# Attention scores: two 64x64 products on opposite quarters of the TensorE array in place of one 128-row product with zero-padded q

## The chip, the cores and the metric

The kernel runs on one core of one Trainium2 chip. The metric is the device time of one execution in microseconds (us). The core has five engines with their own instruction queues: TensorE (PE, with its weight loads shown apart as PEld), VectorE (DVE), ScalarE (ACT), GpSimd (POOL) and SyncE (SP), which here only issues DMAs.

## The reference, cut to what matters

Three layers are chained: a windowed attention, a routed layer with one expert per token, and a second routed layer with two experts per token. Only the attention is touched by the change:

```python
B, H, S, D = q.shape                      # 4, 8, 576, 64
scores = scale * np.matmul(q, k.transpose(0, 1, 3, 2))
mask_plain = (rel >= 0) & (rel < 32)                       # heads 0..3
mask_dil = (rel >= 0) & (rel < 128) & (rel % 4 == 0)       # heads 4..7
scores = np.where(masks[None], scores, -1e9)
attn = np.exp(scores - scores.max(-1, keepdims=True))
attn = attn / (attn.sum(-1, keepdims=True) + 1e-9)
return np.matmul(attn, v)
```

All data is fp32.

## The kernel before

**Units.** The attention is cut into 16 units, each one batch and a pair of heads. The 128 partitions of the transposed q and k tiles (`qT`, `kT`) hold 64 channels of the first head and 64 of the second. A unit has 576 positions in 9 blocks of 64 queries; block n needs only 96 keys (`kT[:, 64*n:64*n+96]`). For heads with the dilated mask the positions are reordered, so that the same 64 by 96 blocks serve.

**Stages of a unit.** The class `Attention` has one method for each stage, and the table `plan` in the main function fixes their order on PE, by a string such as `A0 D0 A1 B0 A2 D1 B1 A3 X E X D2` for each turn of the loop:

- `A0` to `A3` (`qk_T`): three PE transposes into a PSUM bank `tp`, then an eviction into `qT` (parts 0 and 1) or `kT` (parts 2 and 3). It works three units ahead of the values. The eviction of q also scales by -0.125.
- `B0`, `B1` (`scores`): five and four score blocks into a PSUM bank `s`; then on DVE one masked add and minimum for each block (L192, two instructions each, into `sm` and `nmax`); then on ACT one exponential for each block (L196), whose sum goes to `ssum`; then DVE makes the reciprocals `rs` (L198, L199) and POOL multiplies by them (L200).
- `D0` to `D2` (`probs_T`): PE transposes the probabilities into a bank `pt`, and ACT (DVE for part 1) evicts them into `pT` (L215, L217).
- `E` (`values`): products with v into `po0` and `po1`; ACT evicts into `xT`.
- `X`: routing work of earlier batches that is put in between (`logits`, `rows`, tables). `rows` transposes tokens into a bank `tp`, copies them to `xr` (two buffers) and writes them to `xs` in DRAM by a DMA on SP.

PE's order is written out by hand. The order on DVE, ACT, POOL and SP is made by the scheduler of the tile framework at build time.

**The zero padding.** Both heads' scores of a block come from one PE product: the stationary operand is q of the block with queries and heads interleaved, 128 columns, in which column (query, head) holds zeros in the other head's 64 rows. So `qT` is `[128, 576, 2]`, its other half is filled with zeros once by POOL (L82, L83; four buffers, two fills each), and each q eviction is two instructions, one for each head's 64 partitions (L176; L174 on ACT for the first two units). The partitions of the scores are (query, head) interleaved; the eviction of `pT` sorts them by head.

**What follows the attention.** `kT`, `qT` and the masks lie in the pool `at_fix`, the loaded q and k in `at_ld`, both at the right end of the on-chip memory. `first_tile` gives this memory to the first expert weights (pool `w_hl_a`, four tiles `whi`, `wlo` of 8 KB per partition), and `P.load(4)` issues their four DMAs of 1 MB each on SP (L494). `reuse_waits="tile"` makes each new tile wait only for the old tiles in its own bytes. After the attention the first layer starts with `logits_l`, `rows_l` and the expert tile `X[0]`, and then the experts of both layers follow with three-pass products (L454 to L456).

Of the kernel before, what the change touches and what calls it, by code (L numbers as in the profile page):

```python
# [8 lines left out]
F32 = mybir.dt.float32  # L9
# [3 lines left out]
ALU = mybir.AluOpType  # L13
AF = mybir.ActivationFunctionType
# [11 lines left out]
class Attention:  # L26
# [7 lines left out]
    def __init__(self, ctx, early, tc, bank, q, k, v, ident, xT):  # L34
        self.tc, self.nc, self.bank = tc, tc.nc, bank
        self.q, self.k, self.v = q, k, v
        self.ident, self.xT = ident, xT
        self.B, self.H, self.S, self.D = q.shape
        nc = self.nc
        self.NB = self.S // 64  # L40

        self.vp = ctx.enter_context(tc.tile_pool(name="at_v", bufs=2))
        self.wk = ctx.enter_context(tc.tile_pool(name="at_wk", bufs=2))
        fix = early.enter_context(tc.tile_pool(name="at_fix", bufs=1, side="right"))
        self.ld = early.enter_context(tc.tile_pool(name="at_ld", bufs=2, side="right"))
        NB, R = self.NB, self.S // 4


        ip = fix.tile([128, 1], I32, name="ip")
        nc.gpsimd.iota(ip, pattern=[[0, 1]], base=0, channel_multiplier=1)  # L50
        nc.vector.tensor_single_scalar(ip, ip, 1, op=ALU.logical_shift_right)
        fi = fix.tile([128, 2], F32, name="fi")
        nc.vector.tensor_copy(fi[:, 0:1], ip)
        nc.vector.tensor_scalar(fi[:, 1:2], fi[:, 0:1], 32.0, None, op0=ALU.add)
        col = fix.tile([128, 96], F32, name="col")
        nc.gpsimd.iota(col, pattern=[[1, 96]], base=0, channel_multiplier=0, allow_small_or_imprecise_dtypes=True)
        inner = fix.tile([128, 96], F32, name="mask_in")
        nc.vector.tensor_scalar(inner, col, fi[:, 0:1], BIG, op0=ALU.is_le, op1=ALU.mult)
        nc.vector.tensor_scalar(col, col, fi[:, 1:2], BIG, op0=ALU.is_gt, op1=ALU.mult)
        nc.vector.tensor_max(inner, inner, col)  # L60
        first = fix.tile([128, 96], F32, name="mask_first")
        nc.vector.tensor_copy(first, inner)
        nc.vector.memset(first[:, :32], BIG)
        self.mask = [[first] + [inner] * (NB - 1), [first] + [inner] * (NB - 1)]
        rowbig = fix.tile([128, 1], F32, name="rowbig")
        for n in range(1, NB):
            for b in range(R, self.S, R):
                i0, c0 = b - 64 * n, b - 64 * n + 32
                if c0 <= 0 or i0 >= 64:
                    continue  # L70
                m = fix.tile([128, 96], F32, name=f"mask_{n}")
                nc.gpsimd.tensor_copy(m, inner)
                nc.vector.tensor_scalar(rowbig, fi[:, 0:1], float(i0), BIG, op0=ALU.is_ge, op1=ALU.mult)
                nc.vector.tensor_scalar(m[:, :min(c0, 96)], m[:, :min(c0, 96)], rowbig, None, op0=ALU.max)
                self.mask[1][n] = m
        self.kT, self.qT = [], []
        for i in range(4):
            t = fix.tile([128, 32 + self.S], F32, name=f"kT{i}")
            nc.vector.memset(t[:, :32], 0.0)
            self.kT.append(t)  # L80
            t = fix.tile([128, self.S, 2], F32, name=f"qT{i}")
            nc.gpsimd.memset(t[0:64, :, 1], 0.0)  # L82
            nc.gpsimd.memset(t[64:128, :, 0], 0.0)  # L83
            self.qT.append(t)
        self.tiles, self.vt, self.pT, self.p = {}, {}, {}, {}

    def unit(self, m):
# [53 lines left out]
    def qk_T(self, m, part):  # L141

        nc = self.nc
        b, hp, dil = self.unit(m)
        nm, g = "qk"[part // 2], part % 2
        src = self.tiles[nm, m]
        pt = self.bank("tp")[:, :288].rearrange("p (c a) -> p c a", c=3)
        for c in range(3):
            nc.tensor.transpose(pt[:, c, :], src[:, 3 * g + c, :], self.ident[:96, :96])
        if nm == "k":  # L150
            kT = self.kT[m % 4]
            if dil:
                o = kT[:, 32:].rearrange("p (h s c a) -> p h s c a", h=2, s=2, c=3)[:, g]
                i_ = pt.rearrange("p c (a s) -> p s c a", s=2)
            else:
                o = kT[:, 32 + 288 * g:320 + 288 * g]
                i_ = pt.rearrange("p c a -> p (c a)")
            if m < 2 and g == 1:
                nc.scalar.activation(o, i_, AF.Copy)
            else:  # L160
                nc.vector.tensor_copy(o, i_)
            return
        qT = self.qT[m % 4]

        for h in range(2):
            rows = slice(64 * h, 64 * h + 64)
            if dil:
                o = qT[rows, :, h].rearrange("p (h s c a) -> p h s c a", h=2, s=2, c=3)[:, g]
                i_ = pt[rows].rearrange("p c (a s) -> p s c a", s=2)
            else:  # L170
                o = qT[rows, 288 * g:288 * g + 288, h]
                i_ = pt[rows].rearrange("p c a -> p (c a)")
            if m < 2 and h == 1:
                nc.scalar.activation(o, i_, AF.Copy, scale=-0.125)  # L174
            else:
                nc.vector.tensor_scalar(o, i_, -0.125, None, op0=ALU.mult)  # L176

    def scores(self, m, part):
        nc, NB = self.nc, self.NB
        b, hp, dil = self.unit(m)  # L180
        qT, kT = self.qT[m % 4], self.kT[m % 4]
        if part == 0:
            self.p[m] = (self.wk.tile([128, NB, 96], F32, name="sm", bufs=4),
                         [self.wk.tile([128, NB], F32, name=nm, bufs=4) for nm in ("nmax", "ssum", "rs")])
        sm, (nmax, ssum, rs) = self.p[m]
        n0, n1 = ((0, 5), (5, NB))[part]
        ps = self.bank("s")[:, :480].rearrange("p (n c) -> p n c", n=5)
        for n in range(n0, n1):
            nc.tensor.matmul(ps[:, n - n0, :], lhsT=qT[:, 64 * n:64 * n + 64, :].rearrange("p q h -> p (q h)"),
                             rhs=kT[:, 64 * n:64 * n + 96], start=True, stop=True)  # L190
        for n in range(n0, n1):
            nc.vector.tensor_tensor_reduce(out=sm[:, n, :], in0=ps[:, n - n0, :], in1=self.mask[dil][n],  # L192
                                           scale=1.0, scalar=3.0e38, op0=ALU.add, op1=ALU.min,
                                           accum_out=nmax[:, n:n + 1])
        for n in range(n0, n1):
            nc.scalar.activation(sm[:, n, :], sm[:, n, :], AF.Exp, bias=nmax[:, n:n + 1], scale=-1.0,  # L196
                                 accum_out=ssum[:, n:n + 1])
        nc.vector.tensor_scalar(rs[:, n0:n1], ssum[:, n0:n1], 1.0e-9, None, op0=ALU.add)  # L198
        nc.vector.reciprocal(rs[:, n0:n1], rs[:, n0:n1])  # L199
        nc.gpsimd.tensor_tensor(out=sm[:, n0:n1, :], in0=sm[:, n0:n1, :],  # L200
                                in1=rs[:, n0:n1, None].to_broadcast([128, n1 - n0, 96]), op=ALU.mult)

    def probs_T(self, m, part):
        nc, NB = self.nc, self.NB
        if part == 0:
            self.pT[m] = self.wk.tile([96, NB, 128], F32, name="pT", bufs=3)
        p, pT = self.p[m][0], self.pT[m]
        n0 = 3 * part
        pt = self.bank("pt")[:96, :384].rearrange("p (n c) -> p n c", n=3)
        for n in range(n0, n0 + 3):  # L210
            nc.tensor.transpose(pt[:, n - n0, :], p[:, n, :], self.ident)
        o = pT[:, n0:n0 + 3].rearrange("p n (h q) -> p n h q", h=2)
        i_ = pt.rearrange("p n (q h) -> p n h q", h=2)
        if part == 1:
            nc.vector.tensor_copy(o, i_)  # L215
        else:
            nc.scalar.activation(o, i_, AF.Copy)  # L217

    def values(self, m):
        nc, NB, S = self.nc, self.NB, self.S  # L220
# [1441 lines left out]
```

## Time and profile before

| | us |
|---|---|
| median of 3 runs (795.01 to 796.71) | 796.49 |
| the profiled execution, its own time | 798.44 |
| its span in the trace | 796.6 |
| PE busy | 752.0 (94%) |
| DVE busy | 362.3 (45%) |
| ACT busy | 310.3 (39%) |
| POOL busy | 272.8 (34%) |

The span is the time from the first to the last instruction that the profiler recorded; the execution's own time is 1.84 us longer. A busy share over the whole span hides the stages: the attention takes about the first 125 us, and there DVE and ACT are far busier than their averages. PE records overlap (an instruction starts before the one ahead has ended), so a busy share of PE near 100% does not mean that it works at its peak.

### The profile page before, as it was taken

The page shows a single profiled execution, that of the slowest core. Times are in us where ns is not written, and L with a number is a line of the kernel's source. Part 1 is how long each engine was busy: PE and PEld are TensorE (multiplying, and loading weights), DVE is VectorE, ACT ScalarE, POOL GpSimd, SP SyncE. Part 2 cuts the span into 40 slices and gives each one's busy share as a digit, 9 for nine tenths or more (in the row PEclk, how much of TensorE's full clock was granted, in tenths as well). Part 3 has the DMA queues.
Part 4 walks back from the last instruction along what each step waited for, and adds up shares of the span by engine and source line. Part 5 has one row for each costly group of instructions (what it writes and reads, how often), then busy time and mean ns, then how long its engine had stood idle before and what let it go on. Part 6 is the DMA issues. An engine that isn't in the chain of part 4 may idle for free.

```text
span 796.6 us, 13971 instructions
## 1 busy us (share of the span) xinstructions
PE 752.0 (94%) x5280; PEld 647.1 (81%) x5280; DVE 362.3 (45%) x1237; ACT 310.3 (39%) x826; POOL 272.8 (34%) x259
## 2 busy tenths in 40 slices
PE   7998985998998999899999999999999999999994
PEld 7877873866886887789898898997997988988983
DVE  8977894547425636944432441440531531220110
ACT  5778761215214433314433442442532433332120
POOL 6322120024234424134504325434333445544011
PEclk9999997999999999999999999999999999999998
DMA  7978536289679898243725516515445444313122
GB/s 182 182 167 217 127 109 252 68 312 345 247 236 318 294 352 289 70 127 103 202 99 142 142 54 155 130 64 144 130 131 92 118 153 69 115 26 43 17 27 28
DMA packets 109336, 121.06 MB, mean 152 GB/s; under 512 B 42384, under 2 KB 65424, under 8 KB 109264
## 3 DMA queue, kind: packets, MB, share of 16 engines
q1 hardware_dynamic: 98144, 95.95, 38.2%
q0 software_dynamic: 9808, 22.86, 14.7%
q10 hardware_dynamic: 1312, 1.31, 0.5%
q8 instruction: 43, 0.70, 0.4%
q14 instruction: 29, 0.24, 0.1%
HBM read 96.50 MB, written 23.59 MB: 151 GB/s over the span
## 4 chain that ended last, share of the span: by engine, by line
PE 75%; DVE 10%; DMA 5%; ACT 5%; issue 2%; POOL 1%; SPq 0%; POOLq 0%; DVEq 0%; ACTq 0%
PE pt L454 10%; PE pt L456 10%; PE pt L455 10%; PE s L454 5%; PE s L455 5%; PE po L456 5%; PE s L456 5%; PE po L454 5%; PE po L455 5%; ACT sm L196 4%; PE s L755 3%; PE pt L763 3%; PE tp L734 2%; DMA wlo<-in_moe_w_dram 2%; DMA wraw<-in_moe_w_dram 2%
## 5 line engine op out<-in xcount | busy, mean ns | idle before, releaser
L449 POOL TENSOR_TENSOR wlo<-wraw,whi 128x512 fp32r<-128x512 f32 x76 | 109.3, 1497 | 159.2 <-ACT whi L448 139.4
L454 PE MATMUL pt<-whi,hh 128*128 128x512 f32 (+1 forms) x320 | 129.6, 405 | 0.0
L449 DVE TENSOR_TENSOR wlo<-wraw,whi 128x512 fp32r<-128x512 f32 x84 | 79.0, 954 | 110.0 <-ACT whi L448 106.0
L456 PE MATMUL pt<-whi,hl 128*128 128x512 f32 (+1 forms) x320 | 126.1, 394 | 0.0
L455 PE MATMUL pt<-wlo,hh 128*128 128x512 f32 (+1 forms) x320 | 126.0, 394 | 0.0
L448 ACT ACTIVATE whi<-wraw 128x512 fp32r<-128x512 f32 x160 | 91.1, 622 | 57.1 <-PE po L455 17.1
L1224 POOL DMA_INDIRECT out_dram<-y,sidx x40 | 63.3, 1582 | 112.4 <-ACT y L1436 106.8
L727 POOL DMA_INDIRECT xg<-xs,gidx x51 | 52.0, 1019 | 129.4 <-PE tp L734 36.7
L456 PE MATMUL s<-xh,wlo 128*128 128x256 f32 (+1 forms) x256 | 72.7, 284 | 0.0
L455 PE MATMUL s<-xl,whi 128*128 128x256 f32 (+1 forms) x256 | 72.6, 283 | 0.0
L454 PE MATMUL s<-xh,whi 128*128 128x256 f32 (+1 forms) x256 | 72.5, 283 | 0.0
L456 PE MATMUL po<-xh,wlo 128*128 128x352 f32 x224 | 72.5, 324 | 0.0
L454 PE MATMUL po<-xh,whi 128*128 128x352 f32 x224 | 72.4, 323 | 0.0
L455 PE MATMUL po<-xl,whi 128*128 128x352 f32 x224 | 72.2, 322 | 0.0
L456 PEld LDWEIGHTS pt<-whi,hl 128*128 128x128 f32 (+1 forms) x320 | 58.4, 183 | 15.8
L455 PEld LDWEIGHTS pt<-wlo,hh 128*128 128x128 f32 (+1 forms) x320 | 58.6, 183 | 13.7
L454 PEld LDWEIGHTS pt<-whi,hh 128*128 128x128 f32 (+1 forms) x320 | 58.6, 183 | 13.3
L1436 ACT ACTIVATE y<-pt,slots 128x512 f32<-128x512 f32 (+1 forms) x40 | 27.5, 688 | 99.5 <-PE pt L456 88.7
L1422 DVE SCALAR_TENSOR_TENSOR hl<-po,hh 128x352 fp32r<-128x352 f32 x56 | 29.3, 522 | 69.5 <-ACT hh L1421 69.4
L196 ACT ACTIVATE sm<-sm,nmax 128x96 f32<-128x96 f32 x144 | 51.9, 361 | 22.3 <-DVE nmax L192 22.0
L449 DVE TENSOR_TENSOR xl<-tp,xh 128x512 fp32r<-128x512 f32 (+1 forms) x40 | 26.4, 663 | 70.2 <-ACT xh L448 54.5
L200 POOL TENSOR_TENSOR sm<-sm,rs 128x480 f32<-128x480 f32 (+1 forms) x32 | 29.2, 912 | 76.9 <-DVE nmax L192 51.3
(406 smaller groups left out, 1506.8 us busy)
## 6 DMA issues: line engine op xcount, KB each, us to landing
wraw<-in_moe_w_dram SPq DMA_DIRECT2D x40, 1024.0 KB, 5.5
whi<-in_moe_w_dram SPq DMA_DIRECT2D x12, 1024.0 KB, 7.6
wlo<-in_moe_w_dram SPq DMA_DIRECT2D x12, 1024.0 KB, 9.7
out_dram<-zt SPq DMA_DIRECT2D x46, 128.0 KB, 4.3
xs<-xr SPq DMA_DIRECT2D x13, 256.0 KB, 3.2
v<-in_v_dram SPq DMA_DIRECT2D x7, 432.0 KB, 5.4
xs<-xg SPq DMA_DIRECT2D x11, 256.0 KB, 4.4
qld<-in_q_dram SPq DMA_DIRECT2D x8, 288.0 KB, 3.5
```

The costliest lines, as they stand in the source:

```text
L196: nc.scalar.activation(sm[:, n, :], sm[:, n, :], AF.Exp, bias=nmax[:, n:n + 1], scale=-1.0, accum_out=ssum[:, n:n + 1])
L200: nc.gpsimd.tensor_tensor(out=sm[:, n0:n1, :], in0=sm[:, n0:n1, :], in1=rs[:, n0:n1, None].to_broadcast([128, n1 - n0, 96]), op=ALU.mult)
L448: nc.scalar.activation(hi, src, AF.Copy)
L449: (eng or nc.vector).tensor_tensor(out=lo, in0=src, in1=hi.bitcast(F32), op=ALU.subtract)
L454: nc.tensor.matmul(out, lhsT=a[0], rhs=b[0], start=start, stop=False)
L455: nc.tensor.matmul(out, lhsT=a[0], rhs=b[1], start=False, stop=False)
L456: nc.tensor.matmul(out, lhsT=a[1], rhs=b[0], start=False, stop=stop)
L727: gather.last = nc.gpsimd.indirect_dma_start(out=xg, out_offset=None, in_=xs[:n, :], in_offset=bass.IndirectOffsetOnAxis(ap=idx, axis=0))
L755: nc.tensor.matmul(ph[:, 128 * f:128 * f + 128], lhsT=w[:, c, 128 * f:128 * f + 128], rhs=self.x[:, c], start=c == 0, stop=c == KC - 1)
L1224: s = nc.gpsimd.indirect_dma_start(out=out, out_offset=bass.IndirectOffsetOnAxis(ap=idx, axis=0), in_=y, in_offset=None, compute_op=ALU.add)
L1422: nc.vector.scalar_tensor_tensor(hl[1][:, f, s_], in0=ph, scalar=0.0, in1=hl[0][:, f, s_].bitcast(F32), op0=ALU.max, op1=ALU.subtract)
L1436: nc.scalar.activation(y[:n], py, AF.Copy, scale=slots2[:n, 2, j:j + 1])
```

## The change

Each score block is made by two products, one per head: rows 0 to 63 of q and k into partitions 0 to 63 of the bank, and rows 64 to 127 into partitions 64 to 127. The partitions of the scores are now sorted by head, so the query of a partition is its number modulo 64, and the sorting at the eviction of `pT` goes. `qT` shrinks from `[128, 576, 2]` to `[128, 576]`, the zero fills go, and q is evicted by one instruction over 128 partitions, like k.

```diff
-        nc.vector.tensor_single_scalar(ip, ip, 1, op=ALU.logical_shift_right)
+        nc.vector.tensor_single_scalar(ip, ip, 63, op=ALU.bitwise_and)
...
-            t = fix.tile([128, self.S, 2], F32, name=f"qT{i}")
-            nc.gpsimd.memset(t[0:64, :, 1], 0.0)
-            nc.gpsimd.memset(t[64:128, :, 0], 0.0)
-            self.qT.append(t)
+            self.qT.append(fix.tile([128, self.S], F32, name=f"qT{i}"))
...
-        for h in range(2):
-            rows = slice(64 * h, 64 * h + 64)
-            if dil:
-                o = qT[rows, :, h].rearrange("p (h s c a) -> p h s c a", h=2, s=2, c=3)[:, g]
-                i_ = pt[rows].rearrange("p c (a s) -> p s c a", s=2)
-            else:
-                o = qT[rows, 288 * g:288 * g + 288, h]
-                i_ = pt[rows].rearrange("p c a -> p (c a)")
-            if m < 2 and h == 1:
-                nc.scalar.activation(o, i_, AF.Copy, scale=-0.125)
-            else:
-                nc.vector.tensor_scalar(o, i_, -0.125, None, op0=ALU.mult)
+        t = self.kT[m % 4][:, 32:] if nm == "k" else self.qT[m % 4]
+        if dil:
+            o = t.rearrange("p (h s c a) -> p h s c a", h=2, s=2, c=3)[:, g]
+            i_ = pt.rearrange("p c (a s) -> p s c a", s=2)
+        else:
+            o = t[:, 288 * g:288 * g + 288]
+            i_ = pt.rearrange("p c a -> p (c a)")
+        scale = 1.0 if nm == "k" else -0.125
+        if m < 2 and g == 1:
+            nc.scalar.activation(o, i_, AF.Copy, scale=scale)
+        elif nm == "k":
+            nc.vector.tensor_copy(o, i_)
+        else:
+            nc.vector.tensor_scalar(o, i_, scale, None, op0=ALU.mult)
...
-            nc.tensor.matmul(ps[:, n - n0, :], lhsT=qT[:, 64 * n:64 * n + 64, :].rearrange("p q h -> p (q h)"),
-                             rhs=kT[:, 64 * n:64 * n + 96], start=True, stop=True)
+            for h in range(2):
+                rows = slice(64 * h, 64 * h + 64)
+                nc.tensor.matmul(ps[rows, n - n0, :], lhsT=qT[rows, 64 * n:64 * n + 64], rhs=kT[rows, 64 * n:64 * n + 96],
+                                 start=True, stop=True)
...
-        o = pT[:, n0:n0 + 3].rearrange("p n (h q) -> p n h q", h=2)
-        i_ = pt.rearrange("p n (q h) -> p n h q", h=2)
+        o = pT[:, n0:n0 + 3]
         if part == 1:
-            nc.vector.tensor_copy(o, i_)
+            nc.vector.tensor_copy(o, pt)
         else:
-            nc.scalar.activation(o, i_, AF.Copy)
+            nc.scalar.activation(o, pt, AF.Copy)
```

The scheduler makes the other engines' order anew. Two places matter below. The first is VectorE in the middle of the attention, between the end of one unit's masks and the start of the next unit's: `rs` are the reciprocals, `qT` the q evictions, `sm,nmax` a mask instruction with the minimum behind it. Before:

```order
L161 COPY kT_207<-tp 128x288
L198 TENSOR_SCALAR rs<-ssum 128x4
L199 RECIPROCAL rs<-rs 128x4
L176 TENSOR_SCALAR qT_194<-tp 64x288 x4
L192 ISA sm,nmax<-s,mask_first 128x96
L192 ISA nmax 128x1
```

And now, at the same place:

```order
L158 COPY kT_201<-tp 128x288
L184 TENSOR_SCALAR rs<-ssum 128x4
L185 RECIPROCAL rs<-rs 128x4
L160 TENSOR_SCALAR qT_194<-tp 128x288 x2
L178 ISA sm,nmax<-s,mask_first 128x96
L178 ISA nmax 128x1
```

Four q evictions ahead of the next unit's first mask have become two, and nothing else has moved there.

The second is SyncE's queue at the end of the attention, where the last `v` tile has been loaded, one token tile is written (`xs<-xr`), and the first four weight tiles are issued; the square brackets name the counters on which an instruction waits (`DMAHW` for an earlier DMA, the rest by engine). Before:

```order
L135 DMA v_1965<-in_v_dram 96x2x128 [waits DMAHW1_49]
L687 TENSOR_LOAD eri_a [waits DVE_49]
L827 DMA xs<-xr 128x512 [waits DMAHW2_49,DVE_49]
L494 DMA whi<-in_moe_w_dram 128x4x512 [waits DMAHW3_49,DVE_49]
...
L494 DMA wlo<-in_moe_w_dram 128x4x512 [waits DMAHW4_49,PE_49]
...
L494 DMA whi<-in_moe_w_dram 128x4x512 [waits DMAHW5_49]
...
L494 DMA wlo<-in_moe_w_dram 128x4x512 [waits DMAHW6_49,PE_49]
L827 DMA xs<-xr 128x512 [waits DMAHW7_49,DVE_49]
```

And now:

```order
L132 DMA v_2060<-in_v_dram 96x2x128 [waits DMAHW1_49]
L812 DMA xs<-xr 128x512 [waits DMAHW2_49,DVE_49]
L672 TENSOR_LOAD eri_a [waits DVE_49]
L479 DMA whi<-in_moe_w_dram 128x4x512 [waits DMAHW3_49,PE_49]
...
L479 DMA wlo<-in_moe_w_dram 128x4x512 [waits DMAHW4_49]
...
L479 DMA whi<-in_moe_w_dram 128x4x512 [waits DMAHW5_49,DVE_49,Pool_49]
...
L479 DMA wlo<-in_moe_w_dram 128x4x512 [waits DMAHW6_49,PE_49]
L812 DMA xs<-xr 128x512 [waits DMAHW7_49,DVE_49]
```

The DVE wait, which stood on the first weight tile, now stands on the third. The smaller `qT` moves the other tiles of `at_fix` and `at_ld` by 9,216 bytes per partition, while the weight tiles stay where they were: the first weight tile's bytes held the masks and some of `kld`, `kT` and `qT`, and now they hold only loaded q and k; the third now covers the masks. The DVE wait is that for the last mask instruction of the last unit (L192); the PE wait of the first tile is now that for the last transposes of a loaded k tile.

## Rows read from the trace of the kernel before

**Rows 1.** Windows of the whole core: us, busy time of each engine, clock, DMA.

```profile
core 0: us, PE busy (x) PEld busy (x) DVE busy (x) ACT busy (x) POOL busy (x), PEclk, DMA share, GB/s
0.00:116.30 116.30, 102.81 (x1263) 91.48 (x1263) 96.19 (x556) 83.32 (x355) 37.39 (x78) 0.99 0.70 164
116.30:134.00 17.70, 8.40 (x128) 6.79 (x131) 9.45 (x50) 3.99 (x13) 3.02 (x3) 0.83 0.78 282
134.00:796.60 662.60, 640.78 (x3892) 548.84 (x3892) 256.63 (x634) 223.00 (x459) 232.37 (x178) 0.98 0.50 146
```

**Rows 2.** Windows of 10 us in the attention, with the same columns.

```profile
10.00:20.00 10.00, 7.46 (x56) 6.96 (x55) 8.23 (x53) 7.55 (x38) 3.37 (x8) 0.83 0.64 154
30.00:40.00 10.00, 9.63 (x134) 9.05 (x133) 8.79 (x47) 8.12 (x36) 3.38 (x5) 1.00 1.10 205
```

**Rows 3.** The chain that ended last, to 116.3 us, shares by line.

```profile
by line: ACT sm L196 28.0%; PE s L189 9.7%; DVE qT L176 9.6%; PE tp L149 6.1%; DVE sm L192 5.6%; PE pt L211 3.9%; issue 3.6%; ACT xT L251 2.6%; DVE rs L198 2.3%; PE po L247 1.8%; PE tp L833 1.7%; PE tp L821 1.6%; POOL qT L83 1.6%; PE tp L84
```

**Rows 4.** The same chain in order of time: start, us, what.

```profile
8.45 0.62 POOL qT L83
9.09 1.52 DVE mask L74
10.68 1.90 ACT sm L196 x10
...
114.00 1.91 ACT sm L196 x10
```

**Rows 5.** Groups by line and shape, 0 to 200 us: busy us, mean ns.

```profile
L189 PE MATMUL s<-kT,qT 128*128 128x96 f32 x288 | 37.8, 278 | 0.0
L176 DVE TENSOR_SCALAR qT<-tp 64x288 f32<-64x288 f32 x60 | 27.2, 454 | 7.8 <-PE tp L149 6.7
L161 DVE COPY kT<-tp 128x288 f32<-128x288 f32 x30 | 13.5, 451 | 0.0
L82 POOL MEMSET qT<- 64x576 f32 x4 | 2.6, 646 | 0.1
```

**Rows 6.** Timeline of one unit's scores: start us, us, engine, line.

```profile
57.39 1.88 DVE L176 TENSOR_SCALAR qT<-tp 64x288 f32<-64x288 f32 x4 [1.19 <-PE tp L149]
57.52 0.41 PE L149 MATMUL tp<-ident,qld 96*128 96x96 f32 x3
57.77 1.28 PE L189 MATMUL s<-kT,qT 128*128 128x96 f32 x10
58.88 0.41 PE L149 MATMUL tp<-ident,kld 96*128 96x96 f32 x3
59.30 0.26 DVE L192 CUSTOM_DVE_ANT_0 sm<-s,mask_first 128x96 f32<-128x96 f32 x1
59.60 0.38 ACT L196 ACTIVATE sm<-sm,nmax 128x96 f32<-128x96 f32 x1 [1.33 <-DVE nmax L192]
```

**Rows 7.** Timeline of PE around the values of one unit.

```profile
38.97 0.41 PE L149 MATMUL tp<-ident,kld 96*128 96x96 f32 x3
39.31 1.27 PE L229 MATMUL po<-pT,v 96*64 96x64 f32 x36
40.51 0.53 PE L211 MATMUL pt<-ident,sm 128*96 128x128 f32 x3
```

**Rows 8.** Timeline of SP and DVE at the attention's end.

```profile
112.07 0.36 SPq L827 DMA_DIRECT2D xs<-xr  x1
116.29 0.43 SPq L494 DMA_DIRECT2D whi<-in_moe_w_dram  x1
121.04 13.78 SPq L827 DMA_DIRECT2D xs<-xr  x4
...
116.01 0.25 DVE L192 CUSTOM_DVE_ANT_0 sm<-s,mask_in 128x96 f32<-128x96 f32 x1
...
133.16 1.31 DVE L826 COPY xr<-tp 128x512 f32<-128x512 f32 x2 [7.43 <-DMA xs<-xr]
```

More of the change, by code (lines that the diff above doesn't have):

```diff
@@ L149, in qk_T @@
             nc.tensor.transpose(pt[:, c, :], src[:, 3 * g + c, :], self.ident[:96, :96])
-        if nm == "k":
-            kT = self.kT[m % 4]
-            if dil:
-                o = kT[:, 32:].rearrange("p (h s c a) -> p h s c a", h=2, s=2, c=3)[:, g]
-                i_ = pt.rearrange("p c (a s) -> p s c a", s=2)
-            else:
-                o = kT[:, 32 + 288 * g:320 + 288 * g]
-                i_ = pt.rearrange("p c a -> p (c a)")
-            if m < 2 and g == 1:
-                nc.scalar.activation(o, i_, AF.Copy)
-            else:
-                nc.vector.tensor_copy(o, i_)
-            return
-        qT = self.qT[m % 4]
-        for h in range(2):
-            rows = slice(64 * h, 64 * h + 64)
-            if dil:
-                o = qT[rows, :, h].rearrange("p (h s c a) -> p h s c a", h=2, s=2, c=3)[:, g]
-                i_ = pt[rows].rearrange("p c (a s) -> p s c a", s=2)
-            else:
-                o = qT[rows, 288 * g:288 * g + 288, h]
-                i_ = pt[rows].rearrange("p c a -> p (c a)")
-            if m < 2 and h == 1:
-                nc.scalar.activation(o, i_, AF.Copy, scale=-0.125)
-            else:
-                nc.vector.tensor_scalar(o, i_, -0.125, None, op0=ALU.mult)
+        t = self.kT[m % 4][:, 32:] if nm == "k" else self.qT[m % 4]
[12 more added lines that the diff above has]
+            nc.vector.tensor_scalar(o, i_, scale, None, op0=ALU.mult)
     def scores(self, m, part):
@@ L211, in probs_T @@
             nc.tensor.transpose(pt[:, n - n0, :], p[:, n, :], self.ident)
-        o = pT[:, n0:n0 + 3].rearrange("p n (h q) -> p n h q", h=2)
-        i_ = pt.rearrange("p n (q h) -> p n h q", h=2)
+        o = pT[:, n0:n0 + 3]
         if part == 1:
-            nc.vector.tensor_copy(o, i_)
+            nc.vector.tensor_copy(o, pt)
         else:
-            nc.scalar.activation(o, i_, AF.Copy)
+            nc.scalar.activation(o, pt, AF.Copy)
     def values(self, m):
```

## The prediction

> **What bounds the kernel now.** I read first the windows that cut the span at the two places the change can reach [rows 1]. From 134 us on PE is busy 640.8 of 662.6 us with the experts' products, which the change leaves alone: whatever is won or lost must be won or lost before, and is then carried to the end as a shift. To 116.3 us runs the attention, and no engine is full there: PE 102.8, DVE 96.2, ACT 83.3 of 116.3 us. From 116.3 to 134 us PE is busy only 8.4 of 17.7 us.
>
> Then the chain of waits for the attention [rows 3]. It passes from engine to engine: the exponentials on ACT (L196) hold 28%, the score products on PE (L189) 9.7% or 11.3 us, the q evictions on DVE (L176) 9.6% or 11.2 us. The last two are what the change touches. In order of time [rows 4] the first group of exponentials starts at 10.68 us and that of the sixteenth unit at 114.00, so 15 periods of 6.89 us on average.
>
> The timeline of one unit shows how a period closes [rows 6]. The two transposes of q feed four evictions on DVE from 57.39 to 59.27 us; the mask instructions of the new scores stand behind them in DVE's queue and start at 59.30; ACT has waited 1.33 us and starts its exponentials at 59.60. PE meanwhile made the five score blocks of this part from 57.77 to 58.88 us.
>
> Last, the attention's end [rows 8]. The first expert weights are issued at 116.29 us, when the last unit's last masks (the row at 116.01) are done. They are four DMAs of 1 MB, and the token tiles issued from 121.04 us queue behind them. DVE waits 7.43 us for the first of these to land and goes on at 133.16, and PE waits for DVE. So the end of the four weight transfers is what starts the rest of the kernel.
>
> **The change, part by part.**
>
> *Start.* The eight zero fills take about 8 x 0.65 us on POOL [rows 5], the last from 8.45 to 9.07 us, and the fills and index rows queued behind them run later still. The mask instruction at 9.09 us on DVE took 1.52 us [rows 4], six times what a mask of the scores takes (0.26 us, [rows 6]), and the first exponential waited for it until 10.68. Now POOL has 5.2 us less to do ahead of it, and the instruction should take some 0.25 us: 1.3 us less. Two of four q evictions leave DVE's queue here, 0.9 us more, but the first scores' own products come at about the same time as now, which eats most of that. I take 1.6 us; bounds 0.3 (the products come as late as the masks do now) and 2.2 (both in full).
>
> *q evictions.* Sixty instructions of 454 ns over 64 partitions become thirty over 128. The k eviction has exactly this shape and takes 451 ns [rows 5], so half of 27.2 us goes, 0.9 us of DVE in each unit. In the unit of [rows 6] the second eviction can start when its transposes end (57.52 + 0.41 = 57.93) and ends at 58.38, 0.9 us before 59.27.
>
> *Score products.* fp32 products run as two passes, so five blocks are ten records: 58.88 - 57.77 = 1.11 us, or 111 ns each [rows 6]; nine blocks take 2.0 us. Now there are twice as many, each with 64 weight columns. The nearest row is that of the values, 64 weight columns with the two column halves in turn: 36 records in 40.51 - 39.31 = 1.20 us, 33 ns each [rows 7]. They move 64 columns where the scores move 96, so the bounds are 33 and 50 ns; I take 40. Then there is the change of array shape: from transposes to values PE took 39.31 - 38.97 = 0.34 us [rows 7] where a transpose part otherwise takes 57.77 - 57.52 = 0.25 [rows 6], so 0.09 us, and each unit gets four more such changes, two for each part. The five blocks then take 20 x 0.040 + 0.09 = 0.89 us in place of 1.11, and PE wins 2.0 - 36 x 0.040 - 0.36 = 0.2 us a unit; without the cost of the changes and at 33 ns it would be 0.8 us.
>
> *A period.* The masks need the last product of their part. It ends at 57.77 + 0.89 plus a record's tail of 0.17 (1.28 - 1.11), about 58.85 us, which is later than the evictions (58.38). So the masks start 0.45 us earlier, and everything behind them with them. ACT has room: in 30 to 40 us, its fullest stretch, it is busy 8.12 of 10 us [rows 2], so a period of 5.9 us could lose 1.1. I take 0.45 us for all 15 periods, 6.8 us. Bounds: 0.2 (PE sets all of them) gives 3.0, and 0.75 (DVE sets them, products at 33 ns) gives 11.0. The chain gives a check: half of its 11.2 us of evictions and a fifth of its 11.3 us of score products are 7.9 us, a little of which other waits will take back.
>
> *Other edits.* The mask's index costs the same instruction. The eviction of pT reads in another order over the same elements; I take nothing for it.
>
> *Weights.* With the smaller `qT` the first two of the four weight DMAs no longer wait for the last masks, only for transposes that are long done, so they follow the token tile issued at 112.07 us, at about 112.5 instead of 116.29 [rows 8]: 3.8 us. The other two still wait for the masks, at 116.2 us, but four transfers and the first tile behind them take 133.16 - 116.29 = 16.9 us, half of that 8.4, so the first two are still moving until 120.9 and no gap opens. The tile that lands at 133.16 is issued at 121.04 and still stands behind the weights when they end 3.8 us earlier. I take 3.8 us. Bounds: 1 (the early pair shares the engines with the late loads of v) and 4.8 (the copy ahead of the tile at 112.07 us moves up too).
>
> *Sum.* 1.6 + 6.8 + 3.8 = 12.2 us. The profiled execution took 798.44 us (span 796.6 and 1.84 around it), 1.95 above the median of the runs; I take the difference from the median: 796.49 - 12.2 = **784.3 us**.
>
> **A rule that speaks against it.** [Rows 7] shows 0.09 us for a change of array shape. The Trainium skill, TensorEngine Tiling (Array Packing), Key Properties, says that changing the tiling mode drains TensorE; if a drain were a record's whole length less its pace, 278 - 111 = 0.17 us, the trace would bear out only half of it. The same page, Gotcha 1: PSUM Pressure, says that different row tiles cannot write the same bank at one time; no row of this kernel shows two row tiles, so what that would do is the second rival below.
>
> **The rivals.**
>
> *Shape changes cost double.* At 0.17 us, the record's length of 278 ns [rows 5] less its pace, PE loses 36 x 0.040 + 0.68 - 2.0 = 0.12 us a unit instead of winning 0.2, and the masks start 0.37 us earlier. For it speaks that four changes stand in each unit; against it the 0.09 us measured. With 0.1 us a period in the mean: 1.6 + 1.5 + 3.8 = 6.9 us, 789.6 us. Chance 0.12.
>
> *The two halves don't overlap (slower).* Both write one PSUM bank, from different row halves. If one waits for the other, a product costs 2 x 33 = 67 ns [rows 7], nine blocks 36 x 0.067 + 0.36 = 2.8 us, and PE, which is busy 9.63 of 10 us in 30 to 40 us [rows 2], needs 0.8 us more a unit: 12 us over 15 periods, less 5.4 from start and weights, is 6.6 slower, 803 us. It decides from 56 ns a product on (36 x 0.056 + 0.36 = 2.36, 0.36 above now; times 15 that eats the 5.4). Against it: they write different partitions, as the values' halves do. Chance 0.06.
>
> *The early weights bring nothing*, because the tiles land no sooner for another reason: 8.4 us, 788.1 us. Chance 0.10.
>
> *The clock falls.* In 10 to 20 us the granted clock is 0.83 of full speed behind a stretch with little PE work (7.46 busy of 10, [rows 2]), while it is 1.00 in 30 to 40 us. With less work in each period PE could drop to its lower level, 1.2 of 2.4 GHz, now and then. At 0.9 over the attention, a tenth of 103 us of PE work, the gain is nearly gone: about 794 to 797 us. Against it: the periods shrink with the work. Chance 0.04.
>
> **How the numbers follow.** The forecast has 0.66, a gain beyond 17 us 0.02. From the bounds, the sum runs from 0.3 + 3.0 + 1.0 = 4.3 to 2.2 + 11.0 + 4.8 = 18 us, 778.5 to 792.2 us. I give 779 to 791.5, which holds the forecast but for its tails and most of the first and third rivals: about 0.8. A measurement of this kernel tells a difference from about 0.2%, 1.6 us. Faster: 0.66 + 0.02 + 0.12 + 0.10 + half of 0.04 = 0.92; same 0.02; slower 0.06.
>
> **What the profile would show.** Right: 30 q evictions of about 450 ns over 128 partitions; no fill of qT, and first exponentials at about 9 us; 20 score records in 0.8 to 0.9 us; periods of about 6.4 us; two weight DMAs issued right behind a token tile and before the last masks, and DVE's wait for the first token tile behind them ending near 121 us. Wrong: score records that start 56 ns apart or more, a clock below 1.00 in the middle of the attention, or the two early weight DMAs issued with the others.

## The result, and the profile after

The changed kernel took 789.38 us (median of five runs, 787.83 to 791.85) beside 796.71 us for the kernel before on the same chip: a ratio of 0.9905, 95% interval 0.9881 to 0.9928. Run once more in a later group it took 786.67 us beside 797.72, 0.9873 (0.9831 to 0.9915). So 7 to 11 us were won where 12.2 were forecast; the time lies in the range given. The profiled execution took 788.40 us, its span is 786.5 (before: 798.44 and 796.6). Three of the thirteen executions of one version below (e7), the profiled one among them, were slower than the rest by 10 us or more, so its median is that of the other ten, and its trace, whose first 65 us ran at half pace, is read behind 90 us.

Windows cut at the same two places as in [rows 1], the end of the last masks and PE's return:

```profile
0.00:109.48 109.48, 99.77 (x1551) 82.40 (x1551) 81.97 (x526) 82.55 (x352) 32.50 (x70) 1.00 0.74 175
109.48:125.00 15.52, 8.35 (x128) 6.74 (x131) 9.40 (x50) 4.26 (x14) 3.03 (x3) 0.86 0.88 321
125.00:786.50 661.50, 640.03 (x3892) 547.20 (x3892) 257.37 (x634) 222.73 (x459) 231.64 (x178) 0.99 0.51 147
```

Of the 10.1 us between the two spans 6.8 lie in the attention and 2.2 in the stretch behind it; the last stretch is 1.1 us shorter, with the same instructions. DVE's work to the end of the attention fell from 96.19 to 81.97 us. The groups that answer to [rows 5], 0 to 200 us:

```profile
L175 PE MATMUL s<-kT,qT 64*64 64x96 f32 x576 | 30.8, 248 | 0.0
L158 DVE COPY kT<-tp 128x288 f32<-128x288 f32 x30 | 13.6, 453 | 0.0
L160 DVE TENSOR_SCALAR qT<-tp 128x288 f32<-128x288 f32 x30 | 13.3, 449 | 9.3 <-PE tp L146 8.6
```

The q evictions did what was forecast: 30 of 449 ns. They wait for PE's transposes a little more than before (9.3 us in all for 7.8). The same unit as in [rows 6], on PE, DVE and ACT:

```profile
51.95 1.04 DVE L160 TENSOR_SCALAR qT<-tp 128x288 f32<-128x288 f32 x2 [1.19 <-PE tp L146]
52.08 0.41 PE L146 MATMUL tp<-ident,qld 96*128 96x96 f32 x3
52.42 1.04 PE L175 MATMUL s<-kT,qT 64*64 64x96 f32 x20
53.39 0.47 PE L146 MATMUL tp<-ident,kld 96*128 96x96 f32 x3
53.62 0.26 DVE L178 CUSTOM_DVE_ANT_0 sm<-s,mask_first 128x96 f32<-128x96 f32 x1 [0.63 <-PE s L175]
53.70 0.49 PE L197 MATMUL pt<-ident,sm 128*96 128x128 f32 x3
53.92 0.37 ACT L182 ACTIVATE sm<-sm,nmax 128x96 f32<-128x96 f32 x1 [1.10 <-DVE nmax L178]
54.12 0.88 PE L175 MATMUL s<-kT,qT 64*64 64x96 f32 x16
54.93 0.47 PE L146 MATMUL tp<-ident,kld 96*128 96x96 f32 x3
55.23 0.60 PE L806 MATMUL tp<-ident,xT 128*128 128x128 f32 x4
```

The mask now waits 0.63 us for the score products where it had waited for evictions. The twenty records took 53.39 - 52.42 = 0.97 us, 48.5 ns each on average. But the sixteen of the second part took 54.93 - 54.12 = 0.81 us, so four records more cost 0.16 us, 41 ns each, and some 0.15 us of a part do not depend on the number of records. The starts of the single records in the trace agree: the two of a pair, one on each quarter, start 5 to 8 ns apart, and the next pair 82 to 83 ns after the first, except for some 0.05 us more behind the first pair and 0.10 behind the last. The q transposes ahead of them had begun 52.42 - 52.08 = 0.34 us earlier, not the 0.25 of [rows 6]. From the second q transposes to the first mask it is 53.62 - 52.08 = 1.54 us; before it was 59.30 - 57.52 = 1.78.

PE is now the full engine. In 30 to 40 us it is busy 10.00 us ([rows 2]: 9.63). The chain of waits up to PE's return, before (to 134 us) and in the change (to 125 us), begins:

```profile
by line: ACT sm L196 24.3%; DMA xs<-xr 9.0%; PE s L189 8.4%; DVE qT L176 8.3%; PE tp L149 5.3%; DVE sm L192 4.9%; PE pt L211 3.4%; issue 3.3%; ACT xT L251 2.3%; DVE rs L198 2.0%; DVE xr L826 1.9%; PE tp L843 1.9%; PE po L247 1.5%; PE tp L83
```

```profile
by line: PE s L175 17.5%; PE tp L146 12.6%; ACT sm L182 12.3%; DMA xs<-xr 12.2%; PE pt L197 8.1%; PE po L214 4.4%; PE po L232 4.4%; DMA qld<-in_q_dram 2.7%; PE tp L828 2.4%; DVE xr L811 2.2%; DVE sm L178 2.2%; PE tp L818 2.1%; PE tp L806 1.
```

PE's lines lead it now in place of the exponentials, and the q evictions hold too little to stand in the part shown. A DMA, the write of token tiles, has 12.2% or 15 us, where it had 9.0% or 12. It acts at two places. One is the attention's end, as before: SP, the last mask, and DVE, which answer to [rows 8]:

```profile
105.99 1.03 SPq L812 DMA_DIRECT2D xs<-xr  x1
108.19 0.44 SPq L479 DMA_DIRECT2D whi<-in_moe_w_dram  x1
108.84 0.39 SPq L479 DMA_DIRECT2D wlo<-in_moe_w_dram  x1
109.58 0.37 SPq L479 DMA_DIRECT2D whi<-in_moe_w_dram  x1
...
109.19 0.25 DVE L178 CUSTOM_DVE_ANT_0 sm<-s,mask_in 128x96 f32<-128x96 f32 x1
...
124.21 1.30 DVE L811 COPY xr<-tp 128x512 f32<-128x512 f32 x2 [5.30 <-DMA xs<-xr]
```

The first weight transfer went out 1.0 us ahead of the last mask, where before it went out 0.3 us behind its start (116.29 for 116.01 us): 1.3 us were won and not 3.8. It stands 2.2 us behind the token tile. Issuing the token tile took 1.03 us of these (0.36 before), and between the two now stands the load of an expert index, which before stood ahead of the token tile. PE, which waits for DVE's copy, before and in the change:

```profile
133.91 1.29 PE L853 MATMUL tp<-xT,wr 128*32 128x320 f32 x6 [8.34 <-DVE xr L826]
```

```profile
124.96 1.29 PE L838 MATMUL tp<-xT,wr 128*32 128x320 f32 x6 [6.20 <-DVE xr L811]
```

The other place is new, in the middle of the attention:

```profile
47.59 8.47 SPq L132 DMA_DIRECT2D v<-in_v_dram  x13
...
60.94 2.89 SPq L812 DMA_DIRECT2D xs<-xr  x2
...
66.29 0.69 DVE L811 COPY xr<-tp 128x512 f32<-128x512 f32 x1 [1.94 <-DMA xs<-xr]
...
67.04 0.47 PE L146 MATMUL tp<-ident,qld 96*128 96x96 f32 x3 [2.46 <-DVE xr L811]
```

DVE's copy of a token tile waits for the write that was issued at 60.94 us to leave one of the two `xr` buffers, and PE waits for the bank that the copy frees. The time between the two copies into this buffer is not what changed: it is 66.29 - 56.90 = 9.39 us with 1.94 of waiting, 7.45 without, and was 70.07 - 62.58 = 7.49. But the write, which before went out 0.2 us after the first of the two copies had ended, now went out 3.3 us after it (the copy ended at 57.6 us): SP was issuing loads with hardly a pause from 44 us on. The exponentials show what this cost. A unit's first group started at 60.44 us where it had been 66.25 (5.8 earlier), the next unit's at 69.52 where it had been 73.70 (4.2 earlier).

One landmark orders all that follows: the start of the first expert product. Before and in the change (32 records each):

```profile
144.74 5.45 PE L755 MATMUL s<-xt,whi 128*128 128x128 f32 x32
```

```profile
136.37 3.82 PE L740 MATMUL s<-xt,whi 128*128 128x128 f32 x32
```

What lies behind it took 645 to 652 us in the profiles of this case whose tokens were routed as the reference routes them, without regard to the edit, so a single profile's span says little below some 5 us. The medians are steadier.

### The profile page after: what moved, and what is told of

The parts are those of the page before. It is cut to its first block, busy times and chain, and to the rows that moved or that the text cites. A ratio compares the mean times of both kernels' runs of the same rounds, so it can differ in the third digit from the quotient of the medians.

```text
span 786.5 us, 14483 instructions
## 1 busy us (share of the span) xinstructions
PE 748.1 (95%) x5568; PEld 636.3 (81%) x5568; DVE 348.7 (44%) x1207; ACT 309.5 (39%) x824; POOL 267.2 (34%) x251
## 4 chain that ended last, share of the span: by engine, by line
PE 84%; DVE 7%; DMA 3%; ACT 3%; issue 1%; POOL 0%; POOLq 0%; DVEq 0%; ACTq 0%
PE pt L439 10%; PE pt L441 10%; PE pt L440 10%; PE s L740 6%; PE pt L748 5%; PE s L439 5%; PE po L441 5%; PE s L440 5%; PE po L439 5%; PE s L441 5%; PE po L440 5%; PE s L175 3%; PE tp L719 2%; PE tp L146 2%; ACT sm L182 2%; DMA xs<-xr 2%
```

## The experiments

"First exp" is the start of the first exponential, "16th" that of the sixteenth unit, "product" the landmark above, all from the timelines, in us; the ratio is to the kernel before.

| | first exp | 16th | product | median | ratio (95%) |
|---|---|---|---|---|---|
| before | 10.67 | 114.00 | 144.74 | 796.71 to 798.24 | |
| change | 9.43 | 107.19 | 136.37 | 789.38 | 0.9905 (0.9881 to 0.9928) |
| change again (e11) | 9.43 | 106.38 | 134.89 | 786.67 | 0.9873 (0.9831 to 0.9915) |
| e1 products only | 10.68 | 113.88 | 144.47 | 793.28 | 0.9966 (0.9947 to 0.9985) |
| e2 evictions only | 9.58 | 106.00 | | | |
| e3 weights late | 9.25 | 106.42 | 136.93 | 787.61 | 0.9901 (0.9879 to 0.9924) |
| e4 three xr buffers | 9.29 | 108.97 | 135.28 | 786.14 | 0.9903 (0.9865 to 0.9941) |
| e5 last tiles own | 9.31 | 105.92 | 126.67 | 780.32 | 0.9792 (0.9761 to 0.9823) |
| e6 fills back | 9.15 | 106.27 | 134.50 | 787.55 | 0.9888 (0.9855 to 0.9920) |
| e7 heads apart | | | | 797.71 | 0.9998 (0.9972 to 1.0023) |
| e8 parts together | 9.43 | 106.52 | 134.29 | 784.17 | 0.9839 (0.9811 to 0.9867) |
| e9 e5 and e8 | 9.29 | 109.03 | 133.88 | 785.58 | 0.9840 (0.9800 to 0.9880) |
| e10 before, own | 10.51 | 115.22 | 135.99 | 787.47 | 0.9872 (0.9831 to 0.9913) |
| e12 own, weights late | 10.17 | 106.14 | 126.88 | 778.29 | 0.9769 (0.9728 to 0.9809) |

The medians lie 649 to 654 us behind the landmark in every row that has one.

**Products alone (e1).** q stays padded, one half for each head:

```diff
-            self.qT.append(fix.tile([128, self.S], F32, name=f"qT{i}"))
+            t = fix.tile([128, 2, self.S], F32, name=f"qT{i}")
+            nc.gpsimd.memset(t[0:64, 1], 0.0)
+            nc.gpsimd.memset(t[64:128, 0], 0.0)
+            self.qT.append(t)
...
-                nc.tensor.matmul(ps[rows, n - n0, :], lhsT=qT[rows, 64 * n:64 * n + 64], rhs=kT[rows, 64 * n:64 * n + 96],
+                nc.tensor.matmul(ps[rows, n - n0, :], lhsT=qT[rows, h, 64 * n:64 * n + 64], rhs=kT[rows, 64 * n:64 * n + 96],
```

> The two 64x64 products alone: q stays zero-padded (each head's half in its own columns), with the eight fills, the two evictions for each transpose group and the late first weights of the kernel before. Theory (the gain comes from the evictions and the start, and the score products win nothing, since 36 records of 49 ns and four more array-shape changes cost what 18 records of 111 ns did): no change from before, 796.5 us, between 795 and 799; score part 0.97 us, masks still start when the fourth eviction ends. Rival (the products carry the gain): 789 to 792 us.

The unit of [rows 6] in this kernel:

```profile
57.44 1.88 DVE L169 TENSOR_SCALAR qT<-tp 64x288 f32<-64x288 f32 x4 [1.19 <-PE tp L149]
57.57 0.41 PE L149 MATMUL tp<-ident,qld 96*128 96x96 f32 x3
57.91 1.04 PE L184 MATMUL s<-kT,qT 64*64 64x96 f32 x20
...
59.35 0.26 DVE L187 CUSTOM_DVE_ANT_0 sm<-s,mask_first 128x96 f32<-128x96 f32 x1
```

The products end at 58.88 us and the mask still starts at 59.35, when the fourth eviction is through (57.44 + 1.88). The sixteenth unit starts where it did before to 0.1 us, and the first expert product to 0.3 us. The median is 3.6 us lower all the same, and 1.7 us below the range expected. The profile has that difference behind the landmark, where the two kernels run the same instructions; why is not settled. So a few us between two medians don't show by themselves that an edit in the attention won them.

**Evictions alone (e2).**

```diff
-            for h in range(2):
-                rows = slice(64 * h, 64 * h + 64)
-                nc.tensor.matmul(ps[rows, n - n0, :], lhsT=qT[rows, 64 * n:64 * n + 64], rhs=kT[rows, 64 * n:64 * n + 96],
-                                 start=True, stop=True)
+            c = min(64 * n, self.S - 128)
+            nc.tensor.matmul(ps[:, n - n0, :], lhsT=qT[:, c:c + 128], rhs=kT[:, 64 * n:64 * n + 96], start=True, stop=True)
```

> The changed kernel with one product of 128 weight columns for each score block in place of two of 64 (the columns are a plain slice of the unpadded q, so the two heads' scores are mixed and the values are not the reference's): evictions, start and weights of the change without its products. Theory (evictions and start carry the gain): as fast as the change, 789.4 us, between 787.5 and 790.5. Rival (the products carry the gain): 795 to 797 us.

Mixed scores send the tokens to other experts, and the whole took 930 us, which compares with nothing; the attention, whose work does not hang on the values, can be read. Its sixteenth unit starts at 106.00 us, ahead of the change itself. In the unit of [rows 6]:

```profile
52.50 0.41 PE L146 MATMUL tp<-ident,qld 96*128 96x96 f32 x3
52.75 1.28 PE L174 MATMUL s<-kT,qT 128*128 128x96 f32 x10
53.86 0.41 PE L146 MATMUL tp<-ident,kld 96*128 96x96 f32 x3
54.11 0.49 PE L195 MATMUL pt<-ident,sm 128*96 128x128 f32 x3
...
55.58 0.66 PE L804 MATMUL tp<-ident,xT 128*128 128x128 f32 x4
...
54.17 0.26 DVE L176 CUSTOM_DVE_ANT_0 sm<-s,mask_first 128x96 f32<-128x96 f32 x1 [0.77 <-PE s L174]
```

Here 1.67 us lie between the second q transposes and the mask, 1.54 in the change, 1.78 before and with the products alone. So the products shorten this stretch by 0.13 us once the evictions are out of the way, and by nothing otherwise. Over the first nine periods, to the tenth unit's first exponential, the kernel before takes 55.58 us (10.67 to 66.25), e1 the same 55.58 (10.68 to 66.26), e2 51.55 (9.58 to 61.13) and the change 51.01 (9.43 to 60.44). The evictions win 4.0 of the 4.6 us there, and the products another 0.54, 0.06 us a period. At the sixteenth unit nothing of that is left (106.00 for 107.19 and 106.38 us): behind the tenth the change meets its new wait for `xr`, and e2, whose copy there waits for nothing, does not.

**Weights late (e3).** The tile keeps its old size, half of it unused; all orders are the same.

```diff
-            self.qT.append(fix.tile([128, self.S], F32, name=f"qT{i}"))
+            self.qT.append(fix.tile([128, 2, self.S], F32, name=f"qT{i}")[:, 0])
```

> The changed kernel with each q tile's memory kept at its old size, half of it unused, so that the masks again lie under the first weight tile and all four weight DMAs wait for the last masks. Theory (the four were issued only 0.6 us apart at the masks' end anyway, so the early release is worth little): 789.4 to 790.9 us, at most 1.5 slower than the change. Rival (the early pair is worth the forecast 3.8 us): 793.2 us.

The last mask starts at 108.42 us here and at 108.38 in the change run again, so the two can be laid side by side: the first weights go out at 108.80 and 107.52 us, and the first product comes at 136.93 and 134.89. The early issue is worth 2.0 us at that place, of which 1.3 are the earlier start; why DVE's copy then went on 0.8 us sooner after it (16.0 us for 16.7) is not settled. The medians (787.61, and 789.38 and 786.67) don't resolve it.

**Three buffers for xr (e4).** `bufs=3` in the pool `rp`.

> The changed kernel with three buffers for the token rows xr in place of two, so that the copy at 66.29 us no longer waits for a write issued at 60.94 us. Theory (about 2 us of the gain are lost at this wait, lead 5.8 us ahead of it and 3.9 behind): 787.4 us, between 786.5 and 788.3. Rival (the lost lead is won back later, since the weights or the last masks close the attention anyway): 789.4 us as the change.

The wait at 66 us is gone: the eleventh unit starts at 67.13 us, in the five runs of the change and its like-ordered versions e3, e5 and e6 at 68.23 to 69.52. That is 1.1 to 2.4 us. But the scheduler, which knows of the third buffer, put routing work on DVE ahead of q evictions later on:

```profile
99.30 0.74 PE L146 MATMUL tp<-ident,qld 96*128 96x96 f32 x3 [3.47 <-DVE qT L160]
```

By the sixteenth unit the kernel is 1.8 to 2.6 us behind the change. It makes that up at the end, where no copy waits. So the median, near the time expected, is not evidence for the theory: what was won at 66 us was lost on the way, and the end gave it back.

**Last tiles with buffers of their own (e5; e12 with late weights, e10 on the kernel before).**

```diff
-        xr = rp.tile([128, DM], F32, name="xr")
+        xr = rp.tile([128, DM], F32, name="xr_own" if t >= 11 else "xr", bufs=2)
```

> The changed kernel in which the last two token tiles before the first expert tile have buffers of their own, so that their copies no longer wait for the write of an earlier token tile, which stands behind the four weight transfers; PE's and ACT's orders are the same, DVE's up to that place too. Theory (that buffer wait, 6.20 us of PE at 124.96 us in the changed kernel and 8.34 before, is what the weight transfers cost here; the early issue only shortened it): PE goes on at about 119 us, the token rows still land behind the weights, and 3 to 6 us come off the time, 783.5 to 786.5 us. Rival (the first expert tile waits for the landed rows anyway): 788 to 790 us, with PE's wait moved to the first gather.

> The changed kernel with own buffers for the last two token tiles and with the q tiles' old memory size, so that all four weight DMAs wait for the last masks. Theory (with the buffer wait gone nothing on the path waits for the first weights' landing at once): 780 to 782 us, as with own buffers alone. Rival (the first two transfers, issued 2 to 3 us earlier, still start the first expert tile): 782.5 to 784 us.

> The kernel before with buffers of their own for the last two token tiles and no other edit. Theory (its 8.34 us of PE idle at 133.91 us is this buffer wait too, so that all but little of it goes): 787 to 789.5 us; the difference to the changed kernel with the same edit (780.3 us) is then what the change wins without its early weights, about 7 to 8 us. Rival (before the change the late weights hold the rest up all the same): 795 to 797 us.

DVE and PE in e5, at the place of the 5.30 us wait:

```profile
114.12 0.69 DVE L811 COPY xr<-tp 128x512 f32<-128x512 f32 x1
114.82 0.68 DVE L811 COPY xr_own<-tp 128x512 f32<-128x512 f32 x1
115.56 0.69 DVE L811 COPY xr_own<-tp 128x512 f32<-128x512 f32 x1
...
126.67 3.82 PE L740 MATMUL s<-xt,whi 128*128 128x128 f32 x32
```

Nothing waits; the first expert product comes 8.2 us before that of the change run again, although the weights still take their time. The wait itself was 6.29 us there, and 0.5 us are older (the sixteenth unit). The remaining 1.4 go with the clock: from PE's return to the first expert product the same instructions take 10.66 us there (124.23 to 134.89) and 9.27 here (117.40 to 126.67). In 120 to 130 us, in and behind the idle stretch, the clock is granted at 0.66 there, much of it at the lower of its two levels (1.2 of 2.4 GHz), and at 1.00 here:

```profile
120.00:130.00 10.00, 5.73 (x39) 3.03 (x39) 3.66 (x8) 0.49 (x1) 0.00 (x0) 0.66 0.37 140
```

```profile
120.00:130.00 10.00, 9.81 (x113) 8.83 (x112) 5.29 (x18) 1.66 (x3) 0.00 (x0) 1.00 0.39 143
```

The gain was larger than expected in e5, and the kernel before wins 10 us by the same edit (e10). With it the four weights may go out late (e12) at no cost: product at 126.88 us for 126.67. So it was not the weights' landing that PE waited for, but two buffers whose writes stood behind them. The change is worth about the same with this wait gone: 787.47 less 780.32 is 7.2 us by medians of two groups of runs, 787.47 less 778.29 (e12) is 9.2 within one group, and the landmark came 9.3 us earlier in e5 than in e10.

**Fills back (e6).** Eight fills of a scrap tile on POOL, where the old ones stood.

> The changed kernel with eight zero fills of 64x576 on POOL at the place of the old ones, into a tile that nothing reads. Theory (a good part of the gain is won in the first 20 us): first exponential near 10.7 us again instead of 9.43, the third unit's near 19.5 instead of 18.15, and 1.0 to 2.5 us more than the change, 790.4 to 791.9 us. Rival (the start is hidden, since the later units run at PE's pace and catch up): 789.4 us.

The first exponential came at 9.15 us, no later than without them. The theory falls: POOL's fills by themselves do not delay the start. (It also varies without regard to the edits: in the table the versions with a single eviction have it from 9.15 to 10.17 us, those with two from 10.51 to 10.68.) The last mask preparation on DVE took 1.52 us from 9.09 on before [rows 4]. In the change, and with the fills back:

```profile
8.07 0.23 DVE L74 TENSOR_SCALAR mask<-mask,rowbig 128x16 f32<-128x16 f32 x1
```

```profile
8.35 0.56 DVE L74 TENSOR_SCALAR mask<-mask,rowbig 128x16 f32<-128x16 f32 x1
```

Before, two q evictions stand ahead of it on DVE, and it starts just as POOL begins a run of short instructions that ends at 10.57 us; the preparation and the seven instructions started behind it on DVE all ended at 10.60 to 10.62. Now the single eviction stands behind it. In e6 it is through before POOL's run, and in the change POOL has no such run there. That POOL's run held it up is argued from these two ends, not shown: in e6 score masks (0.25 us) and a k eviction (0.45) took their usual time beside the same run (9.56 to 10.51 us).

**Heads apart (e7).** The same products, all of one head and then all of the other within a part.

> The changed kernel with the same score products in another order: within a part all blocks of the first head and then all of the second, so that neighbouring products lie on the same quarter of the array. Theory (the quarters overlap and that gives the 48.5 ns pace): records 70 to 100 ns apart, 0.8 to 1.8 us more a unit, 12 to 25 us slower than the change. Rival (the pace is that of loading weights one after the other, whichever quarter they are for): 48.5 ns as before and 789.4 us.

PE behind 90 us:

```profile
91.59 1.59 PE L175 MATMUL s<-kT,qT 64*64 64x96 f32 x20
93.11 0.47 PE L146 MATMUL tp<-ident,kld 96*128 96x96 f32 x3
...
93.84 1.26 PE L175 MATMUL s<-kT,qT 64*64 64x96 f32 x16
95.03 0.47 PE L146 MATMUL tp<-ident,kld 96*128 96x96 f32 x3
```

Twenty records take 1.52 us, 76 ns each on average, where alternating heads take 48.5. Sixteen take 1.19, so four more cost 0.33 us, 82 ns each on one quarter, where they cost 41 each on two. So products on opposite quarters do overlap, although both write one bank: a pair takes no longer than one product alone. The order costs 8.3 to 11.0 us of the median, nearly the whole gain, though less than the 12 expected at least.

**Score parts together (e8), and with own buffers (e9).** `A0 D0 A1 B0 B1 A2 D1 A3 X E X D2`.

> The changed kernel with the two score parts of a unit next to each other on PE (A0 D0 A1 B0 B1 A2 D1 A3 X E X D2), so that a unit has two changes of array shape for them in place of four. Theory (a change costs 0.07 us and PE sets most periods): 0.15 us a unit, some 2 us, 787.5 us. Rivals: PE has slack in most periods, 789.4 us; or the second part's masks come too early and the transposes too late for DVE, 790 to 792 us.

> The changed kernel with both edits that made it faster: buffers of their own for the last two token tiles, and the two score parts next to each other. Theory (they act at different places, the attention's middle and its end): first product of the first expert tile about 1 us before that of the version with own buffers alone (126.67 us), 778 to 780 us. Rival (the 5 us of the second edit were the same wait at the attention's end, met at a luckier moment): no faster than own buffers alone, 780.3 us or more.

e8 was 2.5 to 5.2 us faster than the change by its median, and 0.6 to 2.1 us at the landmark. Its sixteenth unit starts no earlier, so the shape changes saved are not what it won. Its PE waits 1.78 us at the attention's end in place of 6.20, but only after a wait that the change does not have, in e8 and almost the same in e9 (3.61 us):

```profile
110.22 2.08 PE L708 MATMUL po<-r_ones 128*128 128x128 bf16 x18 [3.62 <-ACT xT L217]
```

ACT makes this `xT` (L217) behind the nine exponentials of the last unit there, and in the change ahead of them. With own buffers e8 did not get faster, and e5 alone beats both. Of the 7.2 us that e9's landmark stands behind that of e5, 3.1 are there at the sixteenth unit and 3.6 are this wait, which only the two kernels with the new order have. How much of the 3.1 comes with that order stays open.

**The change again (e11).**

> The changed kernel once more, on the same chip as the others of this group, since the versions with late weights and with the fills came out at 787.6 us and the change at 789.4 in another group. Theory (those edits cost nothing): 786.5 to 788.5 us here. Rival (both made it faster): 789 to 790 us.

786.67 us: late weights and fills cost nothing that these medians can tell.

## Why the prediction was right, and where its sizes were off

*Start: right in size (1.2 us for 1.6), wrong in cause, so the size was luck.* It was to come mostly from POOL's missing fills. e6 has fills and starts as early; e1 keeps the two evictions and the fills and starts as late as before. That leaves the single eviction, though why the preparation took 1.52 us behind two is not shown.

*q evictions: right.* 30 of 449 ns; e2 shows that they carry 4.0 of the 4.6 us won over the first nine periods.

*Score products: this step failed.* "PE wins 0.2 us a unit" took 40 ns a record and 0.09 us for a change of array shape. The pace was right: inside a part a record more costs 41 ns. The change of shape was sized too small. From the second q transposes to the transposes of tokens behind both parts PE takes 55.23 - 52.08 = 3.15 us in the change and 55.58 - 52.50 = 3.08 in e2. Less the records at their pace (36 x 0.041 = 1.48 and 18 x 0.111 = 2.00 us) 1.67 and 1.08 are left, so the four changes cost 0.59 us, 0.15 each. The 0.09 of [rows 7] is only what passes ahead of the first record (52.42 - 52.08 = 0.34 us against 0.25); the rest passes behind the first pair, behind the last and on the way back (53.70 - 53.39 = 0.31 us against 54.11 - 53.86 = 0.25 in e2). PE does not win 0.2 us a unit but loses 0.07. The masks are still 0.13 us earlier than in e2, which gives the 0.06 us a period. An estimate from these rows: a pair saves 0.111 - 0.082 = 0.03 us, so two changes of 0.15 are paid back at about ten pairs, the five blocks of a first part.

The Trainium skill, TensorEngine Tiling (Array Packing), Key Properties, says that a change of the tiling mode drains TensorE. The 0.15 us lie nearer to the 0.17 at which the prediction priced a full drain than to the 0.09 that it took. The prediction's first rival, with that price, gives 789.6 us, nearly the time measured, but that is chance: it has 0.1 us a period and 3.8 for the weights, where some 0.4 and 2.1 were measured. The rival in which the halves wait for each other in the bank is refuted by e7. The Trainium skill, TensorEngine Tiling (Array Packing), Gotcha 1: PSUM Pressure, says that different row tiles cannot access one bank at one time; here no such wait shows, since a pair that writes one bank takes 82 ns, as long as one product alone in e7. Whether the two touch the bank at the very same moment no row shows.

*A period: right on average, by other means.* (107.19 - 9.43)/15 = 6.52 us, in the second run 6.46, for 6.89 before: 0.37 to 0.43 us each, 0.45 forecast. That the average fits is in part luck. The masks of the unit in [rows 6] came 0.24 us earlier and not 0.45, since the products ended later than forecast, and its period is shorter by just that; but one by one the first nine gains run from 0.13 to 1.23 us. Their mean is 0.51 us (9.43 to 60.44 us, before 10.67 to 66.25). Later it is less, where 1.1 to 2.4 us went at the new wait for `xr`: e12, in which that copy waits for nothing, has (106.14 - 10.17)/15 = 6.40 us, 0.49 less than before. The forecast did not ask whether SP would send out the writes as much earlier as the copies came.

*Weights: 3.8 us forecast, 2.0 to 2.1 measured* (PE's wait 8.34 to 6.20 us, e3's landmark). The forecast let them follow the token tile at once; issuing that took 1.03 us, and the load of the expert index now stands between. The reading under it was off too: "the end of the four weight transfers is what starts the rest" holds only through two `xr` buffers. e5 and e12 free those, and then the weights' time no longer matters.

*Sum.* 1.2 + 5.6 to 6.4 + 2.1 is 8.9 to 9.7 us, what PE's return at 124.96 and 124.23 us shows against 133.91. The two medians give 7.3 and 11.1. (In the prediction's upper bound 15 x 0.75 is 11.25 and not 11.0; the range does not hang on it.) *Clock:* 1.00 throughout the attention, as forecast; in 10 to 20 us it rose from 0.83 to 1.00.

## What to carry to other kernels

Splitting a zero-padded product over the array's quarters paid here by what feeds it: the evictions that it halves, and hardly the products, whose runs in one shape are too short to cover the changes. When a stage gets shorter, look up which buffers' writes it will now catch still on their way, and what stands ahead of those in the issuing queue. A wait on a DMA behind a big transfer can be a wait for a buffer: two more buffers were worth as much as this whole change. And an average pace hides a fixed cost: take it from two runs of different length.

## What the hardware did that was not expected

fp32 products of 64 by 64 with 96 moving columns start in pairs on opposite quarters, 5 to 8 ns apart, every 82 ns, and on one quarter singly every 82 ns, writing the same bank. A change of array shape cost 0.15 us, more than the gap ahead of the first record tells. Six microseconds without PE work cost nearly 8 (e11), with the clock granted at 0.66 in and behind them. And a mask instruction of 0.23 us took 1.52 when it started 1 us later, beside a busy POOL, but 0.56 with POOL as busy at another moment.
